# Banded attention and an expert layer on one core: values as the stationary operand, and expert slots in steps of 16

## The chip, the cores and the metric

The kernel runs on one core of a Trainium2 chip. The core has a matrix engine (TensorE, PE in the profile, with its weight loads listed as PEld), a vector engine (VectorE, DVE), a scalar engine (ScalarE, ACT), GpSimd (POOL) and a queue engine that mostly issues DMAs (SyncE, SP). Each engine runs its own instructions in program order and waits for the others on semaphores. The metric is device microseconds of one execution; less is better.

## What is computed

Attention with a causal window of 96 tokens and 8 global tokens, and a bias that falls with distance, then a layer of 8 experts, of which each token uses the one with the largest gate logit.

```python
# q, k, v: (4, 8, 768, 64) float32; n_global = 8, n_local = 96
scores = scale * q @ k.T                                  # per batch and head
is_global = pos[None, :] < n_global
is_local  = (rel >= 0) & (rel < n_local)                  # rel = query - key
dist = where(is_global & ~is_local, n_local, abs(rel))
scores = where(is_global | is_local, scores - slope[head] * dist, -1e9)
x = softmax(scores) @ v                                   # to (3072, 512)
e = argmax(x @ w_gate);  g = softmax(x @ w_gate)[e]       # 8 experts
y = g * (relu(x @ w1[e]) @ w2[e])                         # w1 512x1024, w2 1024x512
```

With the given inputs expert 0 has 455 tokens and the others, in falling order, 416, 410, 397, 395, 367, 361 and 271.

## The kernel before

All arithmetic is float32; each matrix product in the source becomes two PE instructions in the profile, each transpose on PE one.

**Attention.** The work is cut into 48 units, in the order batch (4), pair of heads `j` (4), and third of the sequence `c` (3, 256 queries each). Because the window is shorter than 128, a block of 128 queries needs only its own block of 128 keys and the one before; `kA` and `va` hold, for each block, the previous block's keys and values with the 16 first tokens of the sequence put over its first 16. Queries and keys arrive by DMA cut into 32x32 blocks, and VectorE transposes them (`turn_qk`, L409 and L410). POOL makes `kA` (`keys_at`, L374 and L376) and `va` (`turn_v`, L400 and L401).

A unit runs through these steps:

- `scores` (L447): PE computes transposed scores, keys on the partitions, for 8 (own or previous block, head, query block) combinations (6 at the start of a sequence, where there is no previous block). ACT takes the exponential (L461). VectorE multiplies with the mask and bias weights `W` (L467 for the first third, otherwise L472, once for each head).
- `attend` (L478): PE multiplies the exponentials, as the stationary operand, with the values, as the moving operand. The value tiles have a column of ones behind each 64 values, so the sums of the weights come out as column 64 of the product. VectorE takes the reciprocal of 4 numbers per partition (L494, into `recips`, which is later looked at for out-of-range sums) and scales the product into `xr`, tokens on the partitions (L497).
- `turn` (L501): PE transposes the unit's `xr` (two 128x128 transposes, L506) and ACT copies that into `xl`, features on the partitions, for the gate. After the last pair of heads SP stores `xr` to the scratch tensor `x_tok` in HBM (`store`, L228).
- `logits`, `logits_sum`, `gate`, `spread`, `spread_sum` (L513 to L604): the gate and, once a batch is done, the place of each token in its expert's list.

The loop at L718 writes out the order by hand: in step `n`, `scores(n)`, `turn(n - 4)`, `logits(n - 5)`, `attend(n - 2)`, `logits_sum(n - 5)`, then the preparation of the next pair. Expert 0's weights are issued on SP, one piece in two of three steps from 8 to 43 (L727).

**Routing.** Experts 1 to 7 are ranked by their token counts; rank r gets `CAPS[r]` slots. If a count exceeds its slots, or a range test fails, the general path (L1073) computes everything again. Expert 0 has 512 slots in four pieces of 128. The first two are filled from the first three batches, and their work, cut into 16 small pieces (`fill`, `work`), is put between the steps of the routing after attention, where PE would wait. The last two pieces run after that (L1051 to L1056). POOL gathers the tokens of 32 slots with each indirect DMA (`gather`, L253), VectorE turns them (`turn_x`, L260), and the results are scattered to the output by an indirect DMA per 128 slots (`put`, L273).

**Experts 1 to 7** (L1061): `hidden` (L999) computes relu(x w1) with the slots as the moving columns, 64 instructions; `result` (L1017) multiplies with w2. Where the slot count is a multiple of 128 (ranks 5 and 6 with 384, which come last), the result has tokens on the partitions and is scaled and scattered directly. Otherwise it comes out transposed, is copied (L1035), and PE transposes it back in `turn` (L1037), which is called inside the next expert's `hidden`. SP loads the next expert's weights meanwhile (`fetch`, L983).

Of the kernel before, what the change touches and what calls it, by code (L numbers as in the profile page):

```python
# [16 lines left out]
P = 128  # L17
GW = 16
# [3 lines left out]
CAPS = (512, 416, 416, 416, 416, 384, 384, 288)  # L22
ORDER = (0, 1, 2, 3, 4, 7, 5, 6)
NQ = 4
R_MIN = 2.0 ** -100
R_MAX = 2.0 ** 60
# [3 lines left out]
def kernel(  # L30
# [28 lines left out]
    x_tok = nc.dram_tensor("x_tok", (N * NJ, P), F32)  # L59

    w1v = moe_w1.rearrange("e (j k q) f -> j q e k f", j=NJ, q=32)
# [34 lines left out]
    vts = [consts.tile([P, 2 * NB * (D + 1) + P - D - 1], F32, name=f"vt{i}") for i in range(3)]  # L96

    def ones_in(t):
        w = 2 * NB * (D + 1)
        nc.gpsimd.memset(t[:, 0:w].rearrange("p (c w) -> p c w", w=D + 1)[:, :, D:D + 1], 1.0)  # L100
        nc.gpsimd.memset(t[:, w:], 1.0)

    ones_in(vts[0])
# [79 lines left out]
    recips = consts.tile([P, 2 * B * H * NB // 4, 2], F32)  # L183
# [12 lines left out]
    xe_0 = [wp0.tile([P, KC, P], F32, name=f"xe_0{i}") for i in range(2)]  # L196
    CM = max(CAPS[1:])
    xq_s = [wp0.tile([P, CM // 32, P], F32, name=f"xq_s{i}") for i in range(2)]
# [29 lines left out]
    def store(t0, n, xr):  # L228

        for i in range(n):  # L230
            nc.sync.dma_start(x_tok[NJ * (t0 + P * i):NJ * (t0 + P * i + P), :].rearrange("(p j) d -> p (j d)", j=NJ),
                              xr[:, i, :])

    def expert_w1(to, e):
        for j in range(NJ):
            nc.sync.dma_start(to[32 * j:32 * j + 32, :, :, :], w1v[j, :, e, :, :])
# [10 lines left out]
    def rows_of(ps, nm, ns, mw, to_rows):  # L247

        pw = ps.tile([P, NS * TB], F32, tag="m", name="pw" + nm)[:, 0:TB * ns]
        nc.tensor.matmul(pw, lhsT=sel, rhs=mw.rearrange("p s g -> p (s g)"), start=True, stop=True)  # L250
        nc.vector.tensor_scalar(out=to_rows, in0=pw, scalar1=float(NJ), scalar2=j_of[:, 0:1], op0=ALU.mult, op1=ALU.add)

    def gather(xq, cols, n, top=N):  # L253

        for i in range(n):
            nc.gpsimd.indirect_dma_start(out=xq[:, i, :], out_offset=None, in_=x_tok[0:NJ * top, :],  # L256
                                         in_offset=bass.IndirectOffsetOnAxis(ap=cols[:, i:i + 1], axis=0),
                                         bounds_check=NJ * top - 1, oob_is_err=False)
# [6 lines left out]
    def take(p):  # L265
        if p < E:
            r = ORDER[p] - 1
            xqs[p] = xq_s[p % 2]
            gather(xqs[p], rows_s[:, NQ * TB * r:NQ * TB * r + NQ * TB], CAPS[r + 1] // 32)

# [17 lines left out]
    def hidden_0(ph, q, f0, nf):  # L288

        for f in range(nf):  # L290
            c0 = P * (f0 + f)
            for kc in range(KC):
                nc.tensor.matmul(ph[:, P * f:P * f + P], lhsT=w1_0[:, 0, kc, c0:c0 + P], rhs=xe_0[q % 2][:, kc, :],  # L293
                                 start=(kc == 0), stop=(kc == KC - 1))
        nc.scalar.activation(hT_0[q % 2][:, f0:f0 + nf, :], ph.rearrange("p (f s) -> p f s", f=nf), AF.Relu)

    def result_0(po, q, f0, nf, later=None):

        for fc in range(f0, f0 + nf):
            nc.tensor.matmul(po, lhsT=hT_0[q % 2][:, fc, :], rhs=w2_0[:, 0, fc, :],  # L300
                             start=(fc == 0), stop=(fc == FC - 1))
        if f0 + nf == FC:
            scaled(f"y_0_{q}", P, po, gslot_0[q // 2][:, 0, q % 2:q % 2 + 1], idx_0[q // 2][:, 0, q % 2:q % 2 + 1], later)
# [18 lines left out]
    def banded_attention():  # L322
        with ExitStack() as actx:
            mp = actx.enter_context(tc.tile_pool(name="maskb", bufs=1))
            xlp = actx.enter_context(tc.tile_pool(name="xlb", bufs=3))
            xrp = actx.enter_context(tc.tile_pool(name="xrb", bufs=5))
# [10 lines left out]
            VW = D + 1  # L337
            NV = 3
            VT, VA = NB * VW, (NB - 1) * VW
            vas = [vp.tile([P, 2 * VA + P - VW], F32, name=f"va{i}") for i in range(2)]  # L340
            for i, t in enumerate(vts):
                if i > 0:
                    ones_in(t)
            for t in vas:
                nc.gpsimd.memset(t[:, 2 * VA:], 1.0)
# [17 lines left out]
            def load_v(pr):  # L363
                b, j = divmod(pr, NJ)
                vt = vts[pr % NV]
                for h in range(2):
                    (nc.scalar if pr == 0 and h == 0 else nc.sync).dma_start(
                        vt[:, VT * h:VT * h + VT].rearrange("p (c w) -> p c w", w=VW)[:, :, 0:D],
                        v[b, 2 * j + h].rearrange("(c p) d -> p c d", p=P))
# [3 lines left out]
            def keys_at(kT, kA, a0, a1):  # L373
                nc.gpsimd.tensor_copy(out=kA[:, a0:a1, GW:P],  # L374
                                      in_=kT[:, a0 * P:a1 * P].rearrange("p (c t) -> p c t", t=P)[:, :, GW:P])
                nc.gpsimd.tensor_copy(out=kA[:, a0:a1, 0:GW],  # L376
# [18 lines left out]
            def turn_v(pr):  # L395
                vt = vts[pr % NV]
                va = vas[pr % 2]
                to = va[:, 0:2 * VA].rearrange("p (h x) -> p h x", h=2)
                vh = vt[:, 0:2 * VT].rearrange("p (h x) -> p h x", h=2)
                nc.gpsimd.tensor_copy(out=to, in_=vh[:, :, 0:VA])  # L400
                nc.gpsimd.tensor_copy(  # L401
                    out=to[0:GW, :, VW:VA].rearrange("p h (c w) -> p h c w", w=VW),
                    in_=vh[0:GW, :, 0:VW].rearrange("p h (o w) -> p h o w", o=1).to_broadcast([GW, 2, NB - 2, VW]))
                pairs[pr] += [vt, va]

            def turn_qk(pr):
# [4 lines left out]
                keys_at(kT, kA, 0, NB - 1)  # L411
# [29 lines left out]
            xrs = {}  # L441
# [5 lines left out]
            def scores(n):  # L447
                b, j, c = units[n]
                qT, kT, kA, _, _ = pairs[b * NJ + j]
# [11 lines left out]
                nc.scalar.activation(e[:, :, 0:w], ps[:, :, 0:w], AF.Exp, scale=D ** -0.5)  # L461
                if n == 0:
                    turn_first(2, NB, ps_s.tile([P, 2, 512], F32, tag="s", name="first_1"))
                elif c == 1 and b == 0 and j + 1 < NJ:
# [4 lines left out]
                else:  # L469
                    for h in range(2):  # L470
                        eh = e[:, h, :].rearrange("p (t c) -> p t c", t=2)
                        nc.vector.tensor_tensor(  # L472
                            out=eh, in0=eh,
                            in1=W[:, 2 * j + h, P:3 * P].rearrange("p (o c) -> p o c", o=1).to_broadcast([P, 2, 2 * P]),
                            op=ALU.mult)
                st[n] = e

            def attend(n):  # L478
                b, j, c = units[n]
                _, _, _, vt, va = pairs[b * NJ + j]  # L480
# [3 lines left out]
                for t in range(2):  # L484
                    mine = [(m, own) for m, (u, own) in enumerate(bl) if u == t]
                    for h in range(2):
                        for m, own in mine:
                            i = 2 * c + t
                            c0 = VT * h + VW * i if own else VA * h + VW * (i - 1)
                            nc.tensor.matmul(po[:, t, h, :], lhsT=pt[:, h, P * m:P * m + P],  # L490
                                             rhs=(vt if own else va)[:, c0:c0 + P],
                                             start=(m == mine[0][0]), stop=(m == mine[-1][0]))
                r = recips[:, 2 * n:2 * n + 2, :]
                nc.vector.reciprocal(r.rearrange("p t (h o) -> p t h o", o=1), po[:, :, :, D:D + 1])  # L494
                if j == 0:
                    xrs[b, c] = xrp.tile([P, 2, DM], F32, tag="xr", name=f"xr_{b}_{c}")
                nc.vector.tensor_tensor(  # L497
                    out=xrs[b, c][:, :, P * j:P * j + P].rearrange("p t (h d) -> p t h d", h=2), in0=po[:, :, :, 0:D],
                    in1=r.rearrange("p t (h o) -> p t h o", o=1).to_broadcast([P, 2, 2, D]), op=ALU.mult)

            def turn(n):  # L501
                b, j, c = units[n]
                xr = xrs[b, c]
                px = ps_m.tile([P, 2, P], F32, tag="m", name=f"px_{n}")
                for t in range(2):
                    nc.tensor.transpose(px[:, t, :], xr[:, t, P * j:P * j + P], ident)  # L506
                if j == 0:
                    xls[b, c] = xlp.tile([P, KC, 2 * P], F32, tag="xl", name=f"xl_{b}_{c}")
                nc.scalar.copy(out=xls[b, c][:, j, :], in_=px.rearrange("p t c -> p (t c)"))
                if j == NJ - 1:  # L510
                    store(S * b + 2 * P * c, 2, xrs.pop((b, c)))
# [101 lines left out]
            def fetch_0(i):  # L613
                rows_of(ps_m, f"_0{i}", 2, st.pop(("w", i)), rows_0[i])
                for h in (2 * i, 2 * i + 1):
                    gather(xq_0[h % 2], rows_0[i][:, TB * (h % 2):TB * (h % 2) + TB], TB, N - S if i == 0 else N)
# [75 lines left out]
            def fit():  # L692
# [18 lines left out]
            turn_v(0)  # L711
# [3 lines left out]
            weights_0 = [lambda f0=f0: nc.sync.dma_start(w2_0[:, :, f0:f0 + 1, :], w2v[:, 0:1, f0:f0 + 1, :]) for f0 in range(FC)]  # L715
            weights_0 += [lambda e=e, kc=kc: nc.sync.dma_start(w1_0[32 * e:32 * e + 32, :, kc:kc + 1, :], w1v[e, :, 0:1, kc:kc + 1, :])
                          for e in range(NJ) for kc in range(KC)]
            for n in range(nu + 1):  # L718
                if n < nu:
# [7 lines left out]
                    if n % 3 > 0 and 8 <= n < 44:  # L727
# [3 lines left out]
                if 0 <= n - 4 < nu:  # L731
                    turn(n - 4)
                if 0 <= n - 5 < nu:
                    logits(n - 5)
                if 0 <= n - 2 < nu:
                    attend(n - 2)
                if 0 <= n - 5 < nu:
# [400 lines left out]
```

## Time and profile before

| | us |
|---|---|
| median of 3 runs | 604.67 (602.85 to 605.37) |
| the profiled execution | 607.0 |
| its span, from the first to the last instruction | 605.1 |
| mean granted PE clock in it | 0.961 |

The stages of the profiled execution, by the windows of the trace:

| stage | from, to (us) | PE busy | DVE busy | granted clock |
|---|---|---|---|---|
| start | 0 to 13 | little | little | 1.00 |
| attention, 48 units | 13.26 to 184.67 | 165.5 of 171.4 | 128.0 | 1.00 |
| routing, with expert 0's first half between | 184.67 to 226.60 | 41.5 of 41.9 | 16.0 | 0.96 |
| a stretch in which PE issues an instruction every 1.4 us or so | 226.60 to 257.70 | 4.7 of 31.1 | 5.2 | 0.56 |
| rest of expert 0 | 257.70 to 284.60 | 26.0 of 26.9 | 0.8 | 0.88 |
| experts 1 to 7 | 284.60 to 597.30 | 305.5 of 312.7 | 43.2 | 0.99 |

"Busy" is the time in which at least one instruction of the engine was in work. A group line of the profile names the source line, engine, operation, output and inputs; durations there are of single instructions, which overlap on PE, so that for PE the chain of waits (start, length, what) gives the better price. The granted clock is TensorE's, as a share of its full speed.

### The profile page before, as it was taken

Reading aid. Unit: us, or ns where it says so; the run is one execution under the profiler, and the core shown is the slowest. Engines: PE = TensorE matmul, PEld = TensorE weight load, DVE = VectorE, ACT = ScalarE, POOL = GpSimd, SP = SyncE. Lnnn points to the kernel's source line nnn. Section 1 sums busy time; section 2 is a strip of 40 time slices with the busy share of each in tenths; the row PEclk is TensorE's granted clock in tenths of the full one; section 3 lists DMA queues with packets and bytes.
Section 4 is the critical chain, followed back from the end, with each engine's and each line's share of the span. In section 5 each row is a group of like instructions: output and inputs, shape, how many; then the busy total and the mean of one; then the engine's idle time right before and its main releaser. Section 6 shows DMA issues by size and latency. Waiting matters only on the chain.

```text
span 605.1 us, 7929 instructions
## 1 busy us (share of the span) xinstructions
PE 547.9 (91%) x3034; PEld 379.4 (63%) x3034; DVE 199.1 (33%) x526; ACT 101.8 (17%) x193; POOL 179.7 (30%) x228
## 2 busy tenths in 40 slices
PE   4999999999998991199999999999999969999994
PEld 3998888998886851184555555555555747554541
DVE  3877876967851633002001301300301301200000
ACT  2543333333232100010110110110110110100100
POOL 4332224222250177601700730620550450101001
PEclk9999999999998996579999999999999998999999
DMA  9999999989212085107561534642625626401000
GB/s 154 147 166 160 235 175 171 217 132 234 64 55 86 5 204 194 50 7 179 167 139 43 185 81 89 214 97 58 205 59 117 202 48 131 176 1 50 1 18 36
DMA packets 145232, 71.96 MB, mean 119 GB/s; under 512 B 126743, under 2 KB 126747, under 8 KB 145184
## 3 DMA queue, kind: packets, MB, share of 16 engines
q1 hardware_dynamic: 137344, 58.16, 45.9%
q0 software_dynamic: 5312, 12.59, 6.5%
q10 hardware_dynamic: 2528, 0.59, 0.6%
q8 instruction: 26, 0.43, 0.3%
q14 instruction: 22, 0.18, 0.1%
HBM read 59.07 MB, written 12.91 MB: 119 GB/s over the span
## 4 chain that ended last, share of the span: by engine, by line
PE 85%; issue 5%; DVE 4%; DMA 2%; another core or an unknown queue 1%; POOL 1%; SPq 0%; ACT 0%; ACTq 0%; POOLq 0%; DVEq 0%
PE ph L1007 24%; PE po L1033 17%; PE o L490 12%; PE s L458 7%; PE po L1025 7%; PE ph L293 6%; PE po L300 4%; PE px L506 3%; PE pt L1042 1%; PE pq L521 1%; PE pi L598 1%; DMA vt<-in_v_dram 1%; DVE y L282 1%; DMA qb<-in_q_dram 1%
## 5 line engine op out<-in xcount | busy, mean ns | idle before, releaser
L256 POOL DMA_INDIRECT xq_s<-x_tok,rows_s x85 | 85.4, 1004 | 25.9 <-issue 24.4
L274 POOL DMA_INDIRECT out_dram<-y,idx_s x25 | 24.3, 973 | 211.2 <-DVE y L282 208.4
L1007 PE MATMUL ph<-xe,w_second 128*128 128x416 f32 (+2 forms) x256 | 81.9, 479 | 0.0
L1009 ACT ACTIVATE hT<-ph 128x416 f32<-128x416 f32 (+2 forms) x56 | 27.7, 495 | 278.2 <-PE ph L1007 233.5
L490 PE MATMUL o<-vt,e 128*128 128x128 f32 x384 | 72.8, 278 | 0.0
L1035 DVE COPY yT<-po 128x416 f32<-128x416 f32 (+1 forms) x20 | 11.3, 565 | 183.8 <-PE po L1033 183.8
L1007 PEld LDWEIGHTS ph<-xe,w_second 128*128 128x128 f32 x256 | 48.4, 190 | 31.9 <-issue 20.5
L1033 PE MATMUL po<-hT,w_second 128*128 128x416 f32 (+1 forms) x192 | 63.8, 493 | 5.1 <-ACT hT L1009 5.1
L1007 PE MATMUL ph<-xe,w_first 128*128 128x416 f32 (+1 forms) x192 | 66.3, 503 | 0.0
L293 PE MATMUL ph<-xe,w_first 128*128 128x128 f32 x256 | 38.2, 304 | 30.0 <-issue 27.2
L490 PE MATMUL o<-va,e 128*128 128x128 f32 x320 | 62.8, 278 | 0.0
L461 ACT ACTIVATE e<-s 128x1024 f32<-128x1024 f32 (+1 forms) x48 | 45.7, 953 | 95.9 <-PE s L458 48.1
L490 PEld LDWEIGHTS o<-vt,e 128*128 128x128 f32 x384 | 57.6, 194 | 1.6 <-issue 1.2
L1033 PEld LDWEIGHTS po<-hT,w_second 128*128 128x128 f32 x192 | 38.0, 199 | 30.4 <-issue 20.4
L293 PEld LDWEIGHTS ph<-xe,w_first 128*128 128x128 f32 x256 | 35.5, 217 | 32.8 <-issue 29.9
L1007 PEld LDWEIGHTS ph<-xe,w_first 128*128 128x128 f32 x192 | 36.2, 190 | 27.8 <-issue 19.7
L472 DVE TENSOR_TENSOR e<-e,Wb 128x512 f32<-128x512 f32 x64 | 44.4, 736 | 18.7 <-ACT e L461 16.3
L490 PEld LDWEIGHTS o<-va,e 128*128 128x128 f32 x320 | 48.7, 193 | 2.6 <-issue 2.5
L1033 PE MATMUL po<-hT,w_first 128*128 128x416 f32 x128 | 45.0, 512 | 0.0
L458 PE MATMUL s<-qT,kT 64*128 64x128 f32 x384 | 40.6, 290 | 0.9 <-ACT qT L392 0.9
L458 PE MATMUL s<-qT,kA 64*128 64x128 f32 x320 | 35.7, 301 | 2.9 <-POOL kA L376 2.9
L1033 PEld LDWEIGHTS po<-hT,w_first 128*128 128x128 f32 x128 | 24.3, 190 | 20.4 <-issue 20.1
(167 smaller groups left out, 525.0 us busy)
## 6 DMA issues: line engine op xcount, KB each, us to landing
w_second<-in_moe_w_dram SPq DMA_DIRECT2D x16, 512.0 KB, 9.5
w_second<-in_moe_w_dram SPq DMA_DIRECT2D x4, 2048.0 KB
x_tok<-xr SPq DMA_DIRECT2D x24, 256.0 KB, 4.0
w_first<-in_moe_w_dram SPq DMA_DIRECT2D x12, 512.0 KB, 7.8
w_first<-in_moe_w_dram SPq DMA_DIRECT2D x3, 2048.0 KB
vt<-in_v_dram SPq DMA_DIRECT2D x31, 192.0 KB, 4.7
qb<-in_q_dram SPq DMA_DIRECT2D x60, 96.0 KB, 4.1
kb<-in_k_dram SPq DMA_DIRECT2D x60, 96.0 KB, 3.8
```

Source lines behind the costliest of these rows:

```text
L256: nc.gpsimd.indirect_dma_start(out=xq[:, i, :], out_offset=None, in_=x_tok[0:NJ * top, :], in_offset=bass.IndirectOffsetOnAxis(ap=cols[:, ...
L274: p = nc.gpsimd.indirect_dma_start(out=out[:, :], out_offset=bass.IndirectOffsetOnAxis(ap=where, axis=0), in_=y[0:rows, :], in_offset=None ...
L293: nc.tensor.matmul(ph[:, P * f:P * f + P], lhsT=w1_0[:, 0, kc, c0:c0 + P], rhs=xe_0[q % 2][:, kc, :], start=(kc == 0), stop=(kc == KC - 1))
L300: nc.tensor.matmul(po, lhsT=hT_0[q % 2][:, fc, :], rhs=w2_0[:, 0, fc, :], start=(fc == 0), stop=(fc == FC - 1))
L458: nc.tensor.matmul(ps[:, h, P * m:P * m + P], lhsT=lhsT, rhs=qT[r, P * i:P * i + P], start=True, stop=True)
L461: nc.scalar.activation(e[:, :, 0:w], ps[:, :, 0:w], AF.Exp, scale=D ** -0.5)
L472: nc.vector.tensor_tensor(out=eh, in0=eh, in1=W[:, 2 * j + h, P:3 * P].rearrange("p (o c) -> p o c", o=1).to_broadcast([P, 2, 2 * P]), op= ...
L490: nc.tensor.matmul(po[:, t, h, :], lhsT=pt[:, h, P * m:P * m + P], rhs=(vt if own else va)[:, c0:c0 + P], start=(m == mine[0][0]), stop=(m ...
L1007: nc.tensor.matmul(ph[:, 0:C], lhsT=w1t[:, 0, kc, P * fc:P * fc + P], rhs=xe[:, kc, 0:C], start=(kc == 0), stop=(kc == KC - 1))
L1009: nc.scalar.activation(hT[:, fc, 0:C], ph[:, 0:C], AF.Relu)
L1025: nc.tensor.matmul(po, lhsT=hT[:, fc, P * q:P * q + P], rhs=w2t[:, 0, fc, :], start=(fc == 0), stop=(fc == FC - 1))
L1033: nc.tensor.matmul(po[:, 0:C], lhsT=w2t[:, 0, fc, P * dc:P * dc + P], rhs=hT[:, fc, 0:C], start=(fc == 0), stop=(fc == FC - 1))
```

## The change

In attention, the roles of the two operands of the value product are exchanged. The values (64 columns) become the stationary operand and the exponentials the moving one, and the two heads write to the lower and upper 64 partitions of one PSUM tile, so `x` comes out with features on the partitions. The ones column is gone; a product with 64 columns of ones gives the sums, repeated on the 64 partitions of each head. VectorE takes the reciprocal of all of them (128x256 a unit) and multiplies into `xl`, which the gate reads directly; PE's transposes and ACT's copy into `xl` go. For the store, VectorE transposes 32x32 blocks of `xl` into `xt`, and four DMAs per 256 tokens (32 partitions each) write them, in a new order of the features within `x_tok`; expert weights `w1` are read in the order that fits it. The test of the sums' range now uses an accumulated sum of the exponentials and, from ACT, the sum of an exponential that is not zero only where a sum is tiny.

```diff
             def attend(n):
...
+                    for m, own in mine:
+                        i = 2 * c + t
+                        for h in range(2):
+                            nc.tensor.matmul(po[D * h:D * h + D, 0, t, :],
+                                             lhsT=vt[:, h, i, :] if own else va[:, h, i - 1, :],
+                                             rhs=pt[:, h, P * m:P * m + P],
+                                             start=(m == mine[0][0]), stop=(m == mine[-1][0]))
+                if c == 0:
+                    parts = [(pt[:, :, 0:4 * P].rearrange("p h (t c) -> p h t c", t=2)[:, :, :, 0:P], 0), (pt[:, :, P:2 * P], 1)]
+                else:
+                    both = pt.rearrange("p h (t o c) -> p h o t c", t=2, o=2)
+                    parts = [(both[:, :, o, :, :], 0) for o in range(2)]
+                for i, (e, t0) in enumerate(parts):
                     for h in range(2):
-                        for m, own in mine:
-                            i = 2 * c + t
-                            c0 = VT * h + VW * i if own else VA * h + VW * (i - 1)
-                            nc.tensor.matmul(po[:, t, h, :], lhsT=pt[:, h, P * m:P * m + P],
-                                             rhs=(vt if own else va)[:, c0:c0 + P],
-                                             start=(m == mine[0][0]), stop=(m == mine[-1][0]))
-                r = recips[:, 2 * n:2 * n + 2, :]
-                nc.vector.reciprocal(r.rearrange("p t (h o) -> p t h o", o=1), po[:, :, :, D:D + 1])
+                        nc.tensor.matmul(po[D * h:D * h + D, 1, t0:2, :], lhsT=ones[:, 0:D], rhs=e[:, h],
+                                         start=(i == 0), stop=(i == len(parts) - 1))
+                r = rp.tile([P, 2, P], F32, tag="r", name=f"r_{n}")
+                nc.vector.reciprocal(r, po[:, 1, :, :])
...
+                xl = xls[b, c][:, j, :]
+                nc.vector.tensor_tensor(out=xl.rearrange("p (t c) -> p t c", t=2), in0=po[:, 0, :, :], in1=r, op=ALU.mult)
+                nc.scalar.activation(junk, po[:, 1, :, :].rearrange("p t c -> p (t c)"), AF.Exp, scale=-2.0 / S_MIN,
+                                     accum_out=small[:, n:n + 1])
 
             def turn(n):
                 b, j, c = units[n]
-                xr = xrs[b, c]
-                px = ps_m.tile([P, 2, P], F32, tag="m", name=f"px_{n}")
-                for t in range(2):
-                    nc.tensor.transpose(px[:, t, :], xr[:, t, P * j:P * j + P], ident)
...
-                nc.scalar.copy(out=xls[b, c][:, j, :], in_=px.rearrange("p t c -> p (t c)"))
+                nc.vector.transpose(xts[b, c][:, :, j, :], xls[b, c][:, j, :].rearrange("p (c t) -> p c t", t=32))
                 if j == NJ - 1:
-                    store(S * b + 2 * P * c, 2, xrs.pop((b, c)))
+                    store(S * b + 2 * P * c, 2, xts.pop((b, c)).rearrange("p c j d -> p c (j d)"))
```

Around it: the mask multiply takes both heads in one instruction; `keys_at` and `turn_v` move from POOL to ACT, and are called in steps `c == 1` and `c == 2` instead of 0 and 1; `turn(n - 2)` follows `attend(n - 2)`; `logits` runs one step earlier; and expert 0's weights are issued two pieces a step in steps 36 to 43, w1 first.

```diff
-                nc.scalar.activation(e[:, :, 0:w], ps[:, :, 0:w], AF.Exp, scale=D ** -0.5)
+                nc.scalar.activation(e[:, :, 0:w], ps[:, :, 0:w], AF.Exp, scale=D ** -0.5, accum_out=sums[:, n:n + 1])
...
-                    for h in range(2):
-                        eh = e[:, h, :].rearrange("p (t c) -> p t c", t=2)
-                        nc.vector.tensor_tensor(
-                            out=eh, in0=eh,
-                            in1=W[:, 2 * j + h, P:3 * P].rearrange("p (o c) -> p o c", o=1).to_broadcast([P, 2, 2 * P]),
-                            op=ALU.mult)
+                    eh = e.rearrange("p h (t c) -> p h t c", t=2)
+                    nc.vector.tensor_tensor(
+                        out=eh, in0=eh,
+                        in1=W[:, 2 * j:2 * j + 2, P:3 * P].rearrange("p h (o c) -> p h o c", o=1).to_broadcast([P, 2, 2, 2 * P]),
+                        op=ALU.mult)
...
             def keys_at(kT, kA, a0, a1):
-                nc.gpsimd.tensor_copy(out=kA[:, a0:a1, GW:P],
+                nc.scalar.copy(out=kA[:, a0:a1, GW:P],
...
             def turn_v(pr):
...
-                nc.gpsimd.tensor_copy(out=to, in_=vh[:, :, 0:VA])
...
+                nc.scalar.copy(out=va, in_=vt[:, :, 0:NB - 1, :])
...
-                    if n % 3 > 0 and 8 <= n < 44:
+                    if 36 <= n < 44:
+                        weights_0.pop(0)()
                         weights_0.pop(0)()
...
+        rows = x_tok[TB * t0:TB * (t0 + P * n), :].rearrange("(c t a) d -> a t c d", t=32, a=TB)
+        for a in range(TB):
+            nc.sync.dma_start(rows[a], xt[32 * a:32 * a + 32, :, :])
```

In the experts, the slot counts are steps of 16 instead of 32. Expert 0 has 464: its first 256 as before, and the other 208 in one piece through `hidden(0)` and `result(0)`, with one gather less (7 instead of 8). No expert's slots are a multiple of 128 any more, so the results of all of them are transposed back by `turn`, the last expert's after its last product. `w2` comes in four DMAs instead of one.

```diff
-CAPS = (512, 416, 416, 416, 416, 384, 384, 288)
+CAPS = (464, 416, 416, 400, 400, 368, 368, 272)
...
-            for z in range(2, NQ):
-                for f0 in range(0, FC, 4):
-                    hidden_0(ps_h.tile([P, 512], F32, tag="ph", name=f"ph_0_{z}_{f0}"), z, f0, 4)
-            for z in range(2, NQ):
-                po = ps_o.tile([P, DM], F32, tag="po", name=f"po_0_{z}")
-                result_0(po, z, 0, FC)
+            hidden(0)
+            turn = result(0)
...
-            turn = None
             for p in range(1, E):
                 hidden(p, turn)
```

## The prediction

> **What bounds the kernel now.** I read the engines' busy shares first, then busy time in windows, then the chain of waits, then single groups on VectorE.
>
> ```profile
> PE 547.9 (91%) x3034; PEld 379.4 (63%) x3034; DVE 199.1 (33%) x526; ACT 101.8 (17%) x193; POOL 179.7 (30%) x228
> ```
>
> TensorE (PE) is busy 91% of the span and VectorE (DVE) a third. That is an average over stages. By windows (length, then PE, PEld, DVE, ACT, POOL busy with counts, clock, DMA share, GB/s):
>
> ```profile
> 13.26:184.67 171.41, 165.48 (x1676) 149.58 (x1676) 127.95 (x294) 62.66 (x111) 51.08 (x74) 1.00 0.88 159
> 226.60:257.70 31.10, 4.71 (x15) 3.48 (x14) 5.16 (x20) 0.00 (x0) 22.28 (x23) 0.56 0.38 123
> 284.60:597.30 312.70, 305.54 (x940) 172.89 (x940) 43.22 (x118) 27.70 (x56) 83.66 (x84) 0.99 0.38 103
> ```
>
> The first line is attention: PE 97% busy, but DVE already 75%. The second is a hole: PE does 4.7 us of work in 31.1 while POOL issues gathers. The third is experts 1 to 7, bound by PE. In the chain, one attention unit reads:
>
> ```profile
> 28.19 0.87 PE s L458 x12
> 29.06 0.37 PE px L506 x2
> 29.42 1.79 PE o L490 x16
> 31.21 1.09 PE s L458 x16
> ```
>
> Scores, the two transposes of L506, the value product, next scores: nothing but PE. A pair (three units) takes 9.07 us (scores start at 28.19 and at 37.26). The rows that price the change:
>
> ```profile
> L494 DVE RECIPROCAL recips<-o x48: 119/177/184, 20.8 to 184.5; 128x4 f32<-128x4 f32 x48
> L224 DVE RECIPROCAL gates<-se x4: 190/191/192, 67.0 to 199.5; 128x6 f32<-128x6 f32 x4
> L537 DVE COPY L<-pl x12: 164/165/176, 56.8 to 197.8; 128x16 f32<-128x16 f32 x12
> L621 DVE TENSOR_SCALAR early<-c x1: 149/149/149, 171.1 to 171.1; 128x1 f32<-128x1 f32 x1
> L568 DVE TENSOR_REDUCE nk<-pb x4: 172/172/173, 74.2 to 201.9; 128x6 f32<-128x18 f32 x4
> L561 DVE TENSOR_REDUCE pv<-pos x4: 203/203/205, 73.7 to 201.4; 128x6 f32<-128x48 f32 x4
> ```
>
> Each gives minimum/median/maximum ns, then shapes. A reciprocal of 4 numbers takes longer than a copy of 16.
>
> **PE in attention.** Removed: two transposes a unit, 0.37 us by the chain, 48 x 0.37 = 17.8 us. The value product keeps 704 instructions but its stationary side is 64 columns wide, and the two heads write different halves of PSUM. Whether two halves run side by side is not shown for this shape. For it: scores use row halves and four of them start 0.22 us apart (55 ns each, against 106 ns for L490: 74.4 us of the chain over 704); the gate's product L521 uses column quarters, eight of 256 columns in 0.57 us (71 ns), where one alone should take 2 x 106 = 213 ns. Side by side: 704 x 0.055 = 39 us. Added: sums by a ones matrix, 320 instructions of 256 columns and 64 of 128, at 107 and 55 ns: 37.7 us. So PE changes by 39 + 37.7 - 74.4 - 17.8 = -15 us, to 150 us. One after the other: 74.4 + 320 x 0.213 + 64 x 0.106 = 149 for both products, PE +57, to 223 us. I take side by side and keep both ends.
>
> **VectorE in attention.** Four edits.
>
> 1. The reciprocal grows from 128x4 to 128x256, 48 times. This is the unknown. PSUM base: L621 (1 element, 149) and L537 (16, 165) give 148 + 1.05 n. L494 is then 177 - 148 = 29 ns for 4 elements, 7.25 ns each. SBUF base: L568 (18 in, 172) and L561 (48 in, 203) give 153 + 1.03 n, so L224 is 191 - 153 = 38 ns for 6, 6.3 ns each. The excess grows nearly with the count, which speaks for a cost per element; a fixed extra would be 25 ns in one row and 32 in the other. At 256: 0.148 + 256 x 7.25 = 2.00 us by L494; 1.77 us by L224; 1.31 us if only the difference of the two excesses (9 ns over 2 elements) scales; 0.44 us if the 25 ns are fixed and each element costs 1.05 ns. I take 2.00, because L494 is the same instruction on the same tile: 48 x (2.00 - 0.175) = +87.6 us.
>
> The Trainium skill's "VectorE: DVE Perf Modes" (Walkthrough: the 8-slice pipeline) says the reciprocal is an iterative divide with a repeat count of 8. Read as 8 cycles an element at its 0.96 GHz, an estimate from that page, it would be 0.148 + 256 x 8.33 ns = 2.28 us, and the whole forecast 675 us. L494 reads a little under it.
>
> 2. New: a 32x32 transpose of 128x256 per unit. 128x768 takes 0.95 us (L409, L410), 128x128 takes 0.257 (L263), so 0.40 us: 48 x 0.40 = +19.2 us.
>
> 3. The mask multiply of both heads becomes one: two of 512 take 1.29 us end to end; one of 1024, from 0.689 at 512 and 0.958 at 768, is 1.23: 32 x -0.06 = -1.9 us.
>
> 4. The normalising multiply keeps its shape (128x256 from PSUM, 0.424 us): 0.
>
> Sum: 127.95 + 87.6 + 19.2 - 1.9 = 232.9 us. That exceeds PE's 150, and even 223. The work that hid VectorE is gone, and VectorE becomes the bound. Reciprocal, multiply and transpose also depend on each other, with 44 ns between two such now (recip to multiply at 103.69): two gaps, one new, 48 x 2 x 0.044 = 4.2 us. Attention takes 237 us against 171.4: **+65.7 us**. VectorE is in order, so behind each reciprocal stand its multiply and transpose, the next mask multiply and q's and k's transposes. Value product, scores and exponential run two units ahead with two PSUM buffers each, so I add no further wait. PE would idle a third of the time in short gaps; its clock was 1.00 through attention and 0.56 in the hole, where it was busy 15%. I take 1.00: at 0.56, PE's 150 would be 268 us and the bound, +31 on the forecast, which I don't think likely with gaps of a microsecond or two.
>
> **ScalarE and POOL.** Key and value copies move from POOL to ACT: by ACT's own 0.37 us at 256 and 0.59 at 512 (L392), about 0.65 + 0.25 + 0.72 + 0.6 = 2.2 us a pair, 35 us. The copy L509 (48 x 0.37) goes, and a like-sized exponential of the sums comes. ACT reaches about 100 of 237 us. Behind the copies queue the exponentials, which have over a unit of slack while VectorE is the bound: 0. If VectorE were not, 2.2 us a pair still fits. POOL loses 42 us that covered nothing: 0.
>
> **DMAs.** SP issues four stores a unit group instead of two (24 more at about 0.5 us of issue, L231): 12 us spread over 237, hidden. Expert 0's 4 MB move from units 8 to 43 into units 36 to 43, eight units of some 4.9 us: 107 GB/s, where 180 was reached in attention (windows): hidden; at PE's present pace (3.0 us a unit) it would be 175 GB/s, with q and k loads ending just then, at most a few us. Weights of later experts keep their bytes; w2 in four pieces costs three more issues, which SP does while waiting: 0.
>
> **Experts.** Slots: 8 instructions of L1007 take 2.79 us at 416 columns and 1.94 at 288 (chain), 0.83 ns per column. Five experts lose 16 columns over 128 instructions: 5 x 1.70 = -8.5 us. Expert 0's second half: 128 instructions at 112 ns (35 in 3.91 us) plus 13.73 us of L300 is 28.1; after, 128 at 0.176 us (208 columns by the same line) is 22.5: -5.6 us. It adds a turn of two groups, +1.0; expert 6 now needs a turn of three, 1.9 us by expert 5's (515.50 to 517.40). Expert 7 ends with one too: copy 0.53, transposes 0.45, then three scatters at POOL's 1.3 us pitch instead of one after its own scaling: +3.6 at the very end. One gather less in the hole: -1.3. Sum: -8.9 us. The hole itself stays, since POOL's run of gathers stays; what makes PE issue so slowly in it I can't tell. That it goes (at most -25) or doubles I leave as a margin.
>
> **Sum.** 65.7 - 8.9 = +56.8 us. The execution profiled took 607.0 us around its span of 605.1, the runs' median is 604.67; I set the sum on the median: **661 us**.
>
> **Rivals.** (1) The reciprocal has a fixed extra, 0.44 us: VectorE 232.9 - 74.9 = 158, plus 4.2 gaps, against PE's 150: attention 162, -9; experts -8.9: **587 us**, faster. For it: both rows are small, and 25 and 32 ns could be two fixed extras; against it: the excess grows with the count. It decides below 0.63 us a reciprocal, where attention is no longer than now. (2) That, and column halves one after the other: PE 223 becomes the bound, +51.6 - 8.9: **647 us**. Against it: L521 overlaps quarters. (3) Partial cost, 1.31 us: VectorE 199.8, plus 4.2: attention +32.6, **628 us**.
>
> "TensorEngine Tiling (Array Packing)" in the skill (PSUM Bottleneck) warns that packing speeds up TensorE but not what empties PSUM; the 75% of VectorE above is where this case would show it, and no row of before has PE waiting for it.
>
> **Chances.** Forecast 0.68 (between 1.6 and 2.45 us a reciprocal, 643 to 683); rival 3 0.10; rival 2 0.03; rival 1 0.16; 0.03 for a sum near none. About 0.5% is what a measurement of this kernel can tell from no change. Faster 0.17, same 0.03, slower 0.80. The range 618 to 688 holds the forecast with the hole's margin, and rivals 2 and 3. The high end is 9 ns an element (L494's maximum, 184) plus 5 us for PE's overlap.
>
> **What would show it.** Right: RECIPROCAL 128x256 near 2.0 us x48, DVE over 95% busy in attention, PE near 65% there, the value product's instructions at about 55 ns. Wrong: the reciprocal near 0.45 us, PE still the chain of attention. For the experts: 2.68 us per 8 instructions at 400 columns, and three scatters after the last matmul. A run far above a millisecond would mean that the fallback ran.

## The result, and the profile after

The changed kernel takes 706.63 us (median of 4 runs, 705.63 to 706.99) against 605.02 us before in the same comparison: a ratio of 1.167, 95% interval 1.161 to 1.173. Slower was forecast, but 661 us; the time lies above the range of 618 to 688. The profiled execution has a span of 705.2 us against 605.1, so the traces have to account for 100.1 us.

Busy shares of the whole span, from the page of the changed kernel:

```profile
span 705.2 us, 8784 instructions
PE 575.0 (82%) x3354; PEld 397.9 (56%) x3354; DVE 290.4 (41%) x553; ACT 141.9 (20%) x359; POOL 135.4 (19%) x153
```

Windows of the changed kernel (length, then PE, PEld, DVE, ACT, POOL busy with counts, granted clock, DMA share, GB/s): attention, routing with expert 0's first half, the slow stretch, the rest of expert 0.

```profile
13.26:292.90 279.64, 202.89 (x1980) 155.59 (x1977) 214.54 (x305) 101.61 (x267) 8.50 (x8) 0.82 0.48 98
292.90:316.55 23.65, 21.60 (x179) 20.95 (x180) 9.33 (x46) 4.41 (x15) 0.00 (x0) 0.93 0.12 32
316.55:366.80 50.25, 24.16 (x66) 14.79 (x64) 11.27 (x47) 0.83 (x4) 34.99 (x35) 0.75 0.42 136
366.80:386.96 20.16, 20.12 (x99) 19.97 (x100) 1.21 (x4) 1.83 (x6) 0.00 (x0) 0.85 0.31 117
```

Read the first line first: attention went from 171.41 to 279.64 us, +108.2. The other three together are 94.06 us where the same stages took 99.93 before (-5.9), and experts 1 to 7 with the tail take 705.2 - 386.96 = 318.2 us against 320.5 (-2.3). 108.2 - 5.9 - 2.3 = 100.0: the whole loss, and more, is in attention.

In that line VectorE, forecast to be over 95% busy, is busy 214.5 of 279.6 us, 77%. TensorE is busy 73% at a granted clock of 0.82. No engine is full, so something makes them wait for each other. The waits of VectorE and of ScalarE (total us, times, longest):

```profile
DVE e L461 <- ACT e L454: 32.2, 15, 2.2
DVE e L465 <- ACT e L454: 25.0, 16, 2.1
...
ACT junk L503 <- DVE xl L502: 152.4, 43, 7.0
```

VectorE's mask multiplies (L461, L465) wait 57.2 us for ScalarE's exponentials, and ScalarE in its turn waits for VectorE, 43 times in 48 units, at `junk`, the name used here for the new exponential of the sums (L503, after the tile that it writes). The timeline of one unit shows how the two hang together (start, length, engine, line; in brackets the idle time before and who ended it):

```profile
31.20 1.75 DVE L497 RECIPROCAL r<-o 128x256 f32<-128x256 f32 x1
32.98 0.43 DVE L502 TENSOR_TENSOR xl<-o,r 128x256 f32<-128x256 f32 x1
33.44 0.45 DVE L508 STREAM_TRANSPOSE xt<-xl 128x256 f32<-128x256 f32 x1
33.52 0.38 ACT L503 ACTIVATE junk<-o 128x256 f32<-128x256 f32 x1 [3.15 <-DVE xl L502]
33.90 0.65 ACT L371 COPY kA<-kT 128x560 f32<-128x560 f32 x1
34.44 0.26 ACT L373 COPY kA<-kT 128x80 f32<-128x80 f32 x1
34.60 1.02 ACT L454 ACTIVATE e<-s 128x1024 f32<-128x1024 f32 x1
35.75 1.23 DVE L465 TENSOR_TENSOR e<-e,Wb 128x1024 f32<-128x1024 f32 x1 [1.86 <-ACT e L454]
```

ScalarE sits idle for 3.15 us until VectorE's multiply has left the PSUM tile, then does `junk`, then a key copy, and only then the next unit's exponential, for which VectorE has been waiting 1.86 us. It is a ring of two engines: reciprocal, multiply, `junk`, copies, exponential, mask multiply, reciprocal. In a pair's first unit VectorE has the next pair's two transposes to do meanwhile and loses nothing; in the other two it loses 1.86 and 2.20 us, so a pair takes 16.89 us (query and key transposes start at 28.38 and at 45.27).

`junk` does not read what the multiply writes; both only read the same PSUM tile. In the Trainium skill, "PSUM — Partial Sum Buffer" (PSUM bank collisions raise a hardware error) says that two engines must not access one bank and quadrant at the same time, reads included, and that the compiler's scheduler adds dependencies for it. The 152.4 us agree with such an order; that it is the reason of this wait is not shown by a run.

The reciprocal itself (minimum, median and maximum in ns):

```profile
L497 DVE RECIPROCAL r<-o x48: 1694/1751/1758, 20.1 to 291.2; 128x256 f32<-128x256 f32 x48
```

It costs per element, as forecast: (1751 - 148) / 256 = 6.26 ns each.

### The profile page after: what moved, and what is told of

It reads as the page before. It is cut to its first block, busy times and chain, and to the rows that moved or that the text cites. A ratio compares the mean times of both kernels' runs of the same rounds, so it can differ in the third digit from the quotient of the medians.

```text
span 705.2 us, 8784 instructions
## 1 busy us (share of the span) xinstructions
PE 575.0 (82%) x3354; PEld 397.9 (56%) x3354; DVE 290.4 (41%) x553; ACT 141.9 (20%) x359; POOL 135.4 (19%) x153
## 4 chain that ended last, share of the span: by engine, by line
PE 51%; DVE 26%; ACT 10%; another core or an unknown queue 7%; issue 3%; DMA 1%; SPq 0%; DVEq 0%; POOL 0%; ACTq 0%; POOLq 0%
PE po L1041 22%; PE ph L1014 21%; DVE r L497 10%; DVE e L465 4%; ACT e L454 4%; DVE xl L502 3%; PE ph L296 2%; DVE e L461 2%; DVE kT L403 2%; DVE qT L404 2%; PE pt L1050 2%; PE s L451 1%; ACT junk L503 1%; ACT va L395 1%
## 5 line engine op out<-in xcount | busy, mean ns | idle before, releaser
L1014 PE MATMUL ph<-xe,w_first 128*128 128x208 f32 (+3 forms) x256 | 83.4, 490 | 25.9 <-issue 18.6
L1016 ACT ACTIVATE hT<-ph 128x416 f32<-128x416 f32 (+4 forms) x64 | 29.7, 467 | 328.5 <-PE ph L1014 239.6
L1041 PE MATMUL po<-hT,w_second 128*128 128x416 f32 (+3 forms) x256 | 81.4, 479 | 5.9 <-issue 3.2
L497 DVE RECIPROCAL r<-o 128x256 f32<-128x256 f32 x48 | 83.9, 1748 | 1.5 <-PE o L494 1.5
L1014 PE MATMUL ph<-xe,w_second 128*128 128x416 f32 (+3 forms) x256 | 79.7, 470 | 0.0
L1041 PE MATMUL po<-hT,w_first 128*128 128x208 f32 (+3 forms) x256 | 75.5, 456 | 0.0
L277 POOL DMA_INDIRECT out_dram<-y,idx_s x25 | 24.2, 969 | 204.8 <-DVE y L285 200.8
L483 PE MATMUL o<-e,vt 128*64 128x128 f32 x384 | 49.1, 344 | 13.0 <-ACT junk L503 13.0
L494 PE MATMUL o<-e,ones 128*64 128x256 f32 (+1 forms) x384 | 56.7, 426 | 0.0
L503 ACT ACTIVATE junk<-o 128x256 f32<-128x256 f32 x48 | 18.4, 383 | 175.6 <-DVE xl L502 152.4
L465 DVE TENSOR_TENSOR e<-e,Wb 128x1024 f32<-128x1024 f32 x32 | 38.8, 1212 | 26.2 <-ACT e L454 25.0
L483 PE MATMUL o<-e,va 128*64 128x128 f32 x320 | 42.2, 353 | 6.2 <-ACT junk L503 3.7
```

Of the source, the lines that this page charges most:

```text
L277: p = nc.gpsimd.indirect_dma_start(out=out[:, :], out_offset=bass.IndirectOffsetOnAxis(ap=where, axis=0), in_=y[0:rows, :], in_offset=None ...
L465: nc.vector.tensor_tensor(out=eh, in0=eh, in1=W[:, 2 * j:2 * j + 2, P:3 * P].rearrange("p h (o c) -> p h o c", o=1).to_broadcast([P, 2, 2, ...
L483: nc.tensor.matmul(po[D * h:D * h + D, 0, t, :], lhsT=vt[:, h, i, :] if own else va[:, h, i - 1, :], rhs=pt[:, h, P * m:P * m + P], start= ...
L494: nc.tensor.matmul(po[D * h:D * h + D, 1, t0:2, :], lhsT=ones[:, 0:D], rhs=e[:, h], start=(i == 0), stop=(i == len(parts) - 1))
L497: nc.vector.reciprocal(r, po[:, 1, :, :])
L503: nc.scalar.activation(junk, po[:, 1, :, :].rearrange("p t c -> p (t c)"), AF.Exp, scale=-2.0 / S_MIN, accum_out=small[:, n:n + 1])
```

## The experiments

The theory (A): the ring is what turned +65.7 into +108.2, and behind it VectorE's reciprocals are the bound. Rivals: TensorE is late because of its clock (B); only the copies that moved to ScalarE matter (C). The first four variants were measured beside the same runs of the kernel before (median 603.25 us).

**One: `junk` behind the next exponential.** The instruction itself is the same, now in `test_small`.

```diff
-                nc.scalar.activation(junk, po[:, 1, :, :]..., AF.Exp, scale=-2.0 / S_MIN, accum_out=small[:, n:n + 1])
+                po_of[n] = po
...
                     scores(n)
+                if 0 <= n - 3 < nu:
+                    test_small(n - 3)
```

> The changed kernel, with ScalarE's exponential of the sums (L503) issued after the next unit's exponential instead of right behind the normalising multiply. Theory A (ring): L503 waits for VectorE's multiply (43 of 48 times), the next unit's exponential stands behind it on ScalarE, and VectorE's next mask multiply waits for that exponential; VectorE then idles 1.9 and 2.2 us in two of three units. Without it a pair of heads takes VectorE's own 13.1 us and its gaps, about 13.4 instead of 16.88: attention 279.6 - 15 x 3.5 = 227, time 706.6 - 53 = 653 us. Theory B (TensorE is late, because its granted clock is 0.82 in attention): the order on ScalarE changes nothing, 705 us. Theory C (only the key and value copies that moved to ScalarE make the exponentials late): they still stand between two exponentials, so under 10 us is gained, 697 us or more.

Measured: 653.12 us, ratio 1.080 (1.074 to 1.087). Its attention, by windows:

```profile
13.26:240.07 226.81, 178.50 (x1984) 138.75 (x1984) 212.08 (x306) 105.26 (x271) 9.57 (x8) 0.88 0.58 120
```

226.8 us, with VectorE busy 212.1, 94%. In the chain that ended last, one stretch is VectorE alone (start, length, what):

```profile
53.93 1.11 DVE e L465
55.04 1.68 DVE r L497
56.72 0.02 issue
56.74 0.43 DVE xl L502
57.17 0.02 issue
57.20 0.45 DVE xt L513
57.64 1.11 DVE e L465
```

This is the picture that the prediction drew: mask multiply, reciprocal, multiply, transpose, next mask multiply, with gaps of 0.02 us. Over all of attention VectorE still waits 226.8 - 212.1 = 14.7 us. The place of one 0.38 us instruction in ScalarE's order was worth 53 us. B and C both fall.

**Two: key and value copies back on POOL.**

```diff
-                nc.scalar.copy(out=kA[:, a0:a1, GW:P], ...
+                nc.gpsimd.tensor_copy(out=kA[:, a0:a1, GW:P], ...
```

> The changed kernel, with the key and value copies (keys_at, turn_v) back on POOL; L503 stays where it is. Theory A: the copies are 0.7 and 1.27 us of the way from L503 to the exponential, once a pair each, so a pair loses 1.97 us: 15 x 1.97 = 30 us, time 677 us. Theory B: 705 us. Theory C: all of VectorE's idle time goes, 4.06 us a pair, 61 us: 646 us.

Measured: 680.50 us, ratio 1.127 (1.120 to 1.134), 26 us under the changed kernel where 30 were expected, and far from B's 705 and C's 646. The copies are part of the way round the ring, not its cause.

**Three: both.**

> Both edits: L503 behind the next exponential, and the key and value copies on POOL. Theory A: once L503 is out of the way the copies have slack, and it adds nothing: 653 us, within 4 us of the run with L503 alone. Theory B: 705 us. Theory C: as with the copies alone, 646 us.

Measured: 653.09 us, ratio 1.081. With `junk` out of the way the copies have slack and cost nothing.

**Four: the experts' part alone**, on the attention of before.

```diff
-CAPS = (512, 416, 416, 416, 416, 384, 384, 288)
+CAPS = (464, 416, 416, 400, 400, 368, 368, 272)
...
+            hidden(0)
+            turn = result(0)
```

> The kernel before with the part behind attention of the changed one: slot counts, expert 0's second half in one piece, w2 in four DMAs; attention as before. The sum on record says -8.9 us; the windows of the two traces give -5.9 (routing to the end of expert 0) and -2.3 (experts 1 to 7), 8.2 together: 596 to 597 us. Rival: the slow stretch behind routing absorbs the gain, or the attention of before feels the new order: 603 us or more.

Measured: 593.11 us, the median of three runs (591.85 to 598.46; a fourth, not counted, took 600.80), ratio 0.983 (0.976 to 0.991). By that interval it is 6 to 15 us under before, and this half of the sum (-8.9) lies inside.

**Five: the division off VectorE.** ScalarE computes it as exp(-ln(sum)); the copies are on POOL, and the test for tiny sums looks at the accumulated reciprocals, so `junk` in its old form goes.

```diff
+    nc.scalar.preload_act_table_set("natural_log_exp_and_others")
     nc.scalar.activation(warm, warm, AF.Exp)
...
-                nc.vector.reciprocal(r, po[:, 1, :, :])
+                nc.scalar.activation(junk, po[:, 1, :, :]..., AF.Ln)
+                nc.scalar.activation(r..., junk, AF.Exp, scale=-1.0, accum_out=small[:, n:n + 1])
```

> The changed kernel with the division taken off VectorE: ScalarE computes 1/sum as exp(-ln(sum)) from the same 128x256 sums, with one activation table that holds both functions; the sum of these reciprocals takes over the test for tiny sums (so L503 goes), and the key and value copies are on POOL. Everything else, the column halves and the transposes on VectorE too, stays. Theory A (VectorE's 48 reciprocals of 1.75 us are what bounds attention once L503 is out of the way): VectorE falls from 214.5 to about 131 us, TensorE's two products and scores become the bound at 3.0 to 3.3 us a unit, attention 155 to 165 us and the time 653 - 226 + 160 = 587, between 580 and 594 us. Theory B (the new products or TensorE's low clock are the bound behind VectorE): attention stays above 200 us, 625 us or more. If ScalarE's two activations and their wait for TensorE make a ring of their own, a unit takes about 4 us: 620 us.

Measured: 594.53 us, ratio 0.981 (0.975 to 0.986), half a microsecond above what A allowed and far from B; attention is 167.4 us where 155 to 165 were expected. Windows, then a pair in the chain:

```profile
13.26:180.67 167.41, 157.50 (x1984) 124.22 (x1984) 136.36 (x257) 95.51 (x256) 57.49 (x77) 0.98 0.79 161
```

```profile
27.98 1.02 PE o L484 x16
29.00 0.86 PE o L495 x8
29.86 1.09 PE s L452 x16
30.96 1.02 PE o L484 x16
31.98 0.86 PE o L495 x8
32.84 1.09 PE s L452 x16
33.94 0.81 PE o L484 x12
34.74 0.65 PE o L495 x8
35.39 0.87 PE s L452 x12
```

ScalarE's two rows for the division (count, then busy time, mean ns of one, and idle time before it):

```profile
L499 ACT ACTIVATE r<-junk 128x256 f32<-128x256 f32 x48 | 20.0, 417 | 1.5
L498 ACT ACTIVATE junk<-o 128x256 f32<-128x256 f32 x48 | 18.4, 383 | 36.9 <-PE o L495 34.5 <-PE pq L520 2.1
```

Now TensorE is busy 94% of attention at a clock of 0.98, and in the pair shown it is alone in the chain: a pair takes 8.28 us (27.98 to 36.26) against 9.07 before. Sixteen such pairs would be 132 of the 167.4 us; in the rest, TensorE's work for the gate and the tokens' places, VectorE, and loads of keys and values stand in the chain too. The column halves do nearly what the prediction took them to do (L484, 16 instructions in 1.02 us, 64 ns each; 55 were taken, 106 would be no overlap) and so does the product with ones (L495, 107 ns an instruction, 107 taken). The loss is therefore VectorE's reciprocal and the ring around it, not TensorE's part of the change. The Trainium skill's "ScalarE: Activation LUTs" (Table sets: the hidden batching unit) lists one set with both functions; on ScalarE the two take 0.38 and 0.42 us here, where VectorE took 1.75.

**Six to ten: the slow stretch behind routing.** TensorE works 24.2 us of 50.3 in the third window of the changed kernel and 4.7 of 31.1 in the kernel before: 26.1 and 26.4 us are lost. So the stretch does not explain the difference, but would be worth having. The theory here (D) was that it lasts as long as POOL's run of gathers; its rival (E), that it does not.

```diff
-            take(2)
             hidden(0)
             turn = result(0)
+            take(2)
```

> The kernel of the run with only the experts' part changed, but the 13 gathers for the second expert (take(2)) are issued after expert 0 instead of before it, so POOL's unbroken run of indirect DMAs behind routing has 20 instead of 33. Theory D (TensorE and ScalarE are held up towards the end of a long run of indirect DMAs on POOL, and let go some 2 us after it): the slow stretch ends 13 x 1.3 = 17 us sooner: 596 - 17 = 579 us, less if the second run, now in expert 1, holds TensorE up too. Theory E (the stretch has to do with expert 0's second half or the weights that arrive then): no change, 594 to 598 us.

> Both edits on the changed kernel: the division on ScalarE and take(2) after expert 0. Theories A and D: 587 - 17 = 570 us. A without D: 587 us; D without A: 612 us or more.

Measured: 595.11 us (0.983) and 596.55 us (0.984), no gain; but the edit did not do what it was meant to: only the place in the program moved, POOL had nothing to wait for, and its run went on to 252 us. So `take(2)` was put behind expert 1's first product, where POOL waits for expert 0's last scaling, on both attentions, and once with the next pair's transposes moved ahead:

```diff
                 hidden(p, turn)
+                if p == 1:
+                    take(2)
```

> The kernel of the run with only the experts' part changed, but take(2) comes after expert 1's first product, so POOL has to wait for the scaling of expert 0's last result before it issues these 13 gathers. (In the run before, only their place in the text moved: POOL had no wait in between, and its run of indirect DMAs went on to 252 us as before.) Theory D (the slow stretch lasts as long as POOL's run): POOL's run behind routing ends 13 x 1.3 = 17 us sooner, at about 235 us, the stretch with it, and the time is 596 - 17 = 579 us. Theory E (the stretch does not depend on the run): 594 to 598 us.

> The changed kernel with the division on ScalarE, key and value copies on POOL, and take(2) after expert 1's first product. Theory D: 594.5 - 17 = 577 us. Theory E: 593 to 597 us.

> As the run before, and the transposes of the next pair's queries and keys (turn_qk) stand before attend(n - 2) in the step instead of behind it, so that VectorE does them while it waits for the reciprocals. With the division on ScalarE attention is bound by TensorE at 8.28 us a pair, 16 x 8.28 = 132 us, but takes about 167; the chain at a batch's end runs through VectorE's multiply, then its two transposes. If they are what is late, some 1.9 us a batch and a part of the other pairs come back, 3 to 10 us: 567 to 574 us under theory D. If not, as the run before.

Measured: 558.46, 554.52 and 552.75 us, but the kernel before took 560.97 us in that comparison, 42 to 46 us less than in the three ahead of it. The ratios are 0.994 (0.992 to 0.996), 0.986 (0.983 to 0.990) and 0.984 (0.980 to 0.987). D against E can't be read from them. Moving the transposes ahead gained 1.8 us (554.52 to 552.75), under the 3 to 10 expected. A last pair was made to compare with the run without this edit:

> The kernel with only the experts' part changed, once more, beside the next one. The chip of the last three runs took 561.0 us for the kernel before, where the others took 603 to 607, and its traces lack the slow stretch behind routing. With the stretch: 8 to 10 us under before, as it was. Without it: expert 0's and the slots' savings are still there, but TensorE then waits for the gathers of expert 0's second half, which the stretch hid: 2 to 8 us under before.

> The same kernel as act_behind_qk, beside the one with only the experts' part changed. If the chip has the slow stretch: theory D (the stretch lasts as long as POOL's run of gathers) says 594.5 - 17 - 2 = 575 us, some 20 under the kernel beside it; theory E says 592 us, 3 or 4 under it. If the chip has no stretch: 553 us, 2 to 6 under the kernel beside it, and D against E stays open.

Measured, beside 561.35 us: 557.83 us (0.992, 0.990 to 0.995) and 550.00 us (0.981, 0.978 to 0.984). The stretch was missing again. What sets it stays open; `act_behind_qk`, the column halves with the division on ScalarE, is faster than both kernels and than the experts' part alone, by 7.8 us in this comparison. The changed kernel itself was not run on a chip without the stretch.

## Why the prediction was wrong

The step that failed is the one about ScalarE's order. The prediction said that behind the copies "queue the exponentials, which have over a unit of slack while VectorE is the bound: 0", and "so I add no further wait". It counted `junk` by its size ("a like-sized exponential of the sums comes") and did not ask what it waits for and what is queued behind it. It waits for VectorE's multiply, and the next exponential is queued behind it. Waits in attention were put at 4.2 us; they were 279.6 - 214.5 = 65.1, and moving the one instruction took the time from 706.6 to 653.1 us, 8 us under the forecast. That it comes so near is in part luck: in that run VectorE's work in attention was 232.9 - 212.1 = 20.8 us less than forecast, and its waits 14.7 - 4.2 = 10.5 us more.

The other steps:

- **The reciprocal.** Right in kind (a cost per element), 2.00 us forecast, 1.75 measured: L224's reading, which gave 1.77, was the better one. 48 x 0.25 = 12 us too many, which hid part of the missed wait. The estimate from the Trainium skill's "VectorE: DVE Perf Modes" (Walkthrough: the 8-slice pipeline), read as 8 cycles an element, was 2.28; the measured row decides for 1.75.
- **VectorE's other edits.** The transpose took 0.445 us (0.40 forecast, 48 x 0.045 = 2.2 us), the joined mask multiply 1.21 (1.23). VectorE's sum was 214.5 us against 232.9 forecast; the reciprocal's price is 12 of the 18. The mask multiplies of the second and third units are another 4: they kept VectorE busy 44.4 us before and 38.8 after, 5.6 less where 1.9 was forecast. The rest lies in small rows.
- **VectorE as the bound.** Right, but only behind the ring: 94% busy in the first experiment, 77% in the changed kernel.
- **TensorE.** Prices nearly right at full clock: 57 to 64 ns for an instruction of the value product (55 taken), 107 for the ones (107 taken), and 157.5 us busy in experiment five against a forecast of 150. That its clock stays at 1.00 was wrong (0.82). The runs show no cost of that: in experiment one, at 0.88, VectorE was busy 94% of attention. "No row of before has PE waiting for it" was not quite so, since before, TensorE waits 0.8 us at L506 and 1.6 us at L1042 for VectorE instructions that read PSUM (L497, L282); nothing in the forecast hung on it.
- **DMAs.** Nearly right: one DMA stands in the chain of attention, 3.13 us for expert 0's w1 at 219.55 us, and just ahead of it SP takes 2.5 us to issue four stores and a piece of the weights.
- **Experts.** -8.9 forecast, -8.2 by the windows, -10.1 alone (593.11 against 603.25), but only -3.5 on a chip without the slow stretch (557.83 against 561.35, a ratio of 0.992): the forecast held for a chip that has the stretch. Eight instructions at 400 columns take 2.69 us (2.68 forecast). From the last matmul of w2 to the end it is 11.0 us instead of 7.8, +3.2 (+3.6 forecast). The slow stretch stays, as said.
- **The rivals.** All three put the reciprocal lower and none made the order on ScalarE a case: the mechanism that decided had no chance in the forecast, and the range, built on the reciprocal's price alone, could not hold it.

## What to carry to other kernels

When an edit puts a new instruction on an engine that is not the bound, write down what it waits for and what stands behind it before pricing its length: 0.38 us at the wrong place cost 53 us here. Two engines that read the same PSUM tile were kept in an order here, and the second reader could be issued a step later at no cost. And an operation that is cheap at 4 elements has to be priced at the size that a new layout gives it, then compared with another engine: the same division cost VectorE 1.75 us and ScalarE 0.80.

## What the runs showed of the hardware that was not expected

TensorE's granted clock fell after gaps far shorter than the slow stretch. In the changed kernel TensorE is idle from about 43 to 45.55 us; before that gap 16 instructions of the value product start within 0.92 us (39.97 to 40.89), after it 12 take 1.34 us (45.55 to 46.89), 57 and 112 ns each. Three windows, before, in and after the gap:

```profile
38.00:42.80 4.80, 4.80 (x64) 3.59 (x60) 2.53 (x5) 2.50 (x6) 0.00 (x0) 0.98 0.02 4
42.80:45.40 2.60, 0.22 (x4) 0.03 (x2) 2.53 (x4) 0.44 (x2) 0.00 (x0) 0.92 0.00 0
45.40:48.90 3.50, 3.27 (x24) 2.38 (x24) 3.50 (x4) 1.93 (x5) 0.00 (x0) 0.57 0.23 39
```

The Trainium skill, "TensorE: Matmul & The Clock Gate" (Part 1: The HAM clock gate), puts the idle window at about 3.4 us; a gap of 2.5 us was enough in this place.

The kernel before took 603 to 607 us in three comparisons and 561 us in the other two. The four comparisons of the experiments ran on four chips: the traces of two show the slow stretch, those of the other two, with 561 us, do not. In the last one the kernel with only the experts' part changed waits 8.7 us for a gather (216.29 to 224.97) and then works without a break. Its window there:

```profile
226.00:258.00 32.00, 32.00 (x158) 28.67 (x157) 10.10 (x37) 3.79 (x10) 24.41 (x25) 0.95 0.88 251
```

TensorE is busy all of 32 us, while POOL issues gathers for 24 of them and the DMAs move 251 GB/s. Expert 1's first product starts at 249.99 us here. In the first run of experiments six to ten, which differs from it only in the place of `take(2)`, it starts at 274.84 us, on a chip with the stretch; that is 24.9 of the 32.7 us between the two spans (592.6 and 559.9). So the stretch is most of what separates these chips, and neither POOL's run of gathers nor the loads alone make it; what does is open.
